# Stores of the FFT's intermediate results, sent from ScalarE's queue instead of SyncE's

## The chip, the cores and the metric

One core of one Trainium2 chip runs the whole program. A core has TensorE (matrix products into PSUM), VectorE, ScalarE and GpSimd, each with its own instruction queue served in order, and SyncE, which only issues transfers. The metric is the device time of one execution in microseconds; three runs of the kernel before gave 601.61, 601.63 and 604.45 us, median 601.63.

## The reference

Two layers follow each other. The first is a global filter: an FFT along the sequence, a product with a complex filter, and the inverse.

```
x: (8, 2496, 256) float32                      # batch, sequence, channels
X = rfft(x, axis=1); Y = X * (filt_r + 1j*filt_i); y = irfft(Y, n=2496, axis=1)
```

The second is a mixture of eight experts; each of the 19968 tokens goes to one of them.

```
logits = y @ w_gate + modality_bias[modality_id]          # y as 19968 rows of 256
e = argmax(logits); gate = softmax(logits)[e]
out[token] = gate * (relu(y[token] @ w1[e]) @ w2[e])      # w1[e]: 256x1024, w2[e]: 1024x256
```

## The kernel before

The FFT of length 2496 is done as 48 x 52 in matrix products, in three stages for each batch of 2496 tokens.

Stage one (`stage1`, L204) multiplies pieces of x by a 96x96 matrix; ScalarE evicts each result from PSUM into a tile t (L214), and after every second eviction, and after the last of a batch, the tile is stored into the DRAM tensor `b1_d` (L217): seven stores a batch. Stage two loads it back in another layout as t2 (`load_t2`, L449), transforms it (`forward`, L464), evicts it on ScalarE into xf (L496), multiplies it on VectorE by the filter (L503, L504), transforms back (`inverse`, L474), and ScalarE evicts into a tile z (L518); after every second eviction z is stored into `b2_d` (L520): six stores a batch. Stage three loads that as t4 (`load_t4`, L455), does the last products (L564, L567), evicts y into yo (L592 on ScalarE, L594 on VectorE), transposes it (L579) and forms the logits. Tiles t and z have two buffers each: an eviction into one waits until the store of its earlier content has landed.

Then the batch is routed (`count`, `place`, `tabled`), GpSimd scatters its rows into `bins_d`, one bin for each expert (L672), and the experts read blocks of 256 rows from there into xs (`load`, L744; the transfer is L750). A block is transposed (L779), multiplied by w1 (L793) with the result evicted on ScalarE into hT (L798), multiplied by w2 (L806), scaled on VectorE (L813) and scattered by GpSimd into the output (L815).

Batches 0 and 1 keep their intermediate results on the chip. For batch 2 from stage two on, and for batch 3 in stage one, the stores start while the FFT runs alone; this part is written in an order fixed by hand, and the flag `alone` is true in it. From about 120 us on `alone` is false: one loop over steps n (L1117) writes, for each step, stage one of one batch, stage two of the one before, stage three of the one before that, some scatters, and one or two quarter steps of the experts. In this loop the order on each engine is set by the framework's planner: it takes the instructions in the program's order but lets one go ahead that is ready sooner by its own estimate of times. PSUM holds three buffers with the tag `ps`, which all three stages take in turn, and two for `hps`.

SyncE issues all hardware-queue transfers of this loop: the loads of xs, t2 and t4 and the stores of t and z. It goes through them in the planner's order, and one that waits holds those behind it. What a transfer waits for is written into the program by the framework: for a store the eviction; for a load of t2 or t4 the landing of the stores that it reads; for a load of xs a free buffer of five and, for the first blocks of a batch, the landing of that batch's scatters. Each hardware-queue transfer also counts up one of eight semaphores, in turn, and waits for the landing of the transfer that used the same one before, eight transfers ago.

Of the kernel before, what the change touches and what calls it, by code (L numbers as in the profile page):

```python
# [29 lines left out]
def kernel(  # L30
# [12 lines left out]
    nc = tc.nc  # L43
# [49 lines left out]
    b1_d = nc.dram_tensor("b1_d", (B, NTT, KA, D), BF16, kind="Internal").ap()  # L93
    b2_d = nc.dram_tensor("b2_d", (B, NS, KB, D), BF16, kind="Internal").ap()
# [19 lines left out]
    EV = 2  # L114
# [74 lines left out]
    st = [dict() for _ in range(B)]  # L189

    def chunk_of(t):
        for c, (t0, t1) in enumerate(TCH):
            if t0 <= t < t1:
                return c, t0, t1

    alone = [True]

    def front(pool, tag, bufs=None):

        if alone[0]:  # L200
            return pool.tile([P, EV, D], F32, tag=tag, bufs=bufs, name="fp")
        return pp.tile([P, EV, D], F32, tag="ps", name="ps")

    def stage1(g, k):  # L204
        t = k * EV
        c, t0, t1 = chunk_of(t)
        xt = xts[g, c]
        ps = front(hp, "hps")
        for i in range(EV):
            mm = nc.tensor.matmul(ps[:KA, i, :], lhsT=w1m, rhs=xt[:, t - t0 + i, :], start=True, stop=True)  # L210
        marks["pe"].append(mm.ins)
        if k % 2 == 0:
            st[g]["t1"] = rp.tile([KA, 2, EV, D], BF16, tag="t1", bufs=2, name="t1")
        nc.scalar.copy(st[g]["t1"][:, k % 2], ps[:KA])  # L214
        if k % 2 == 1 or k == NP - 1:
            n = (k % 2 + 1) * EV
            nc.sync.dma_start(b1_d[g, t + EV - n:t + EV].rearrange("t p c -> p t c"),  # L217
                              st[g]["t1"].rearrange("p a b d -> p (a b) d")[:, :n])

    def input_piece(g, k):  # L220

        stage1(g, k)
        if (k + 1) * EV in [t1 for t0, t1 in TCH]:
            load_x()
# [78 lines left out]
    with tc.manual_schedule():  # L303
# [102 lines left out]
        for s0 in range(0, NS, SPB):  # L406
            for src, dst in ((w2m, a1m), (w2x, a2m)):
# [8 lines left out]
                a = 0  # L416
                if s0 == 0:
                    nc.scalar.copy(dst[:, 0, :], tp[:KB, 0:KB])
                    a = 1
# [87 lines left out]
    def returned(g, k, pz):  # L507

        s = k * EV
        if g < TURNED:  # L510
            if k == 0:
                st[g]["zT"] = turns.tile([P, DC, NTT, KA], BF16, tag="turn", name="zT")
            nc.scalar.copy(st[g]["zT"][:, :, :, 4 * s:4 * (s + EV)],
                           pz[:, 0:DC * EV * KB].rearrange("p (a u t) -> p a t u", a=DC, t=NTT))
            return
        if k % 2 == 0:
            st[g]["z"] = rp.tile([KB, 2, EV, D], BF16, tag="z", bufs=2, name="z")
        nc.scalar.copy(st[g]["z"][:, k % 2], pz[:KB])  # L518
        if k % 2 == 1:
            nc.sync.dma_start(b2_d[g, s - EV:s + EV].rearrange("s p c -> p s c"),  # L520
                              st[g]["z"].rearrange("p a b d -> p (a b) d"))

    NK = NS // EV

    def stage2(g, k):

        if k < NK:
            ps = forward(g, k)
        if k > 0:
            pz = inverse(g, k - 1)  # L530
        if k < NK:
            filtering(g, k, taken(g, k, ps))
        if k > 0:
            returned(g, k - 1, pz)

    def around(g, k, middle):

        if k < NK:
            xf = taken(g, k, forward(g, k))
        middle(lambda: k < NK and filtering(g, k, xf))  # L540
        if 0 < k <= NK:
            returned(g, k - 1, inverse(g, k - 1))

    def stage3(g, k):
# [12 lines left out]
        if k < NPY:  # L557
            t0 = TCH[k // 3][0]
            t4 = st[g]["t4", k // 3]
            ps = front(op, "ops", 2)  # L560
            for i in range(EV):
                a, b = divmod(u0 + i, 3)
                t = 4 * a + b if u0 < NYF else 4 * NYG + i
                mm = nc.tensor.matmul(ps[:, i, :], lhsT=wbm[:, 0, :], rhs=t4[:, t - t0, :],  # L564
                                      start=True, stop=u0 >= NYF)
                if u0 < NYF:
                    mm = nc.tensor.matmul(ps[:, i, :], lhsT=wbm[:, 1 + b, :], rhs=t4[:, 4 * a + 3 - t0, :],  # L567
                                          start=False, stop=True)
            marks["pe"].append(mm.ins)
# [372 lines left out]
    with tc.manual_schedule(engines={ET.PE, ET.Activation, ET.DVE}):  # L942
# [145 lines left out]
        n = -(NP + 2)  # L1088
# [23 lines left out]
    n = opening[0][1] + WAIT  # L1112
# [3 lines left out]
    n = 0  # L1116
# [78 lines left out]
```

## Time and profile before

| | before |
|---|---|
| median of three runs | 601.63 us |
| profiled execution | 604.51 us, of which 602.5 us span |
| TensorE (PE) busy | 511.2 us, 85% |
| ScalarE (ACT) busy | 380.8 us, 63% |
| VectorE (DVE), GpSimd (POOL) | 374.0 us and 370.6 us, 62% each |
| hardware-queue transfers (SyncE) | 41.45 MB, 26.4% of the DMA engines' time |
| GpSimd's transfers | 50.75 MB, 34.2% |
| stores of t, 192 KB and 96 KB | 30 and 5 |
| stores of z, 208 KB | 36 |

The span runs from the first to the last instruction of the profiled execution. Issuing a transfer does not count as busy, so SyncE has no share. The chain that ended last lies 47% on TensorE, 15% on transfers, 9% on GpSimd, 8% on VectorE and 6% on ScalarE. Instructions are named by the line that made them: "t L214" is the eviction into t.

### The profile page before, as it was taken

How to read it: one execution, taken by the hardware profiler on the slowest of the kernel's cores; microseconds unless marked ns; L12 is line 12 of the kernel's file. 1: busy time of each engine (PE TensorE's matmuls, PEld its weight loads, DVE VectorE, ACT ScalarE, POOL GpSimd, SP SyncE). 2: the span in 40 equal slices, each digit the busy share in tenths (PEclk: the TensorE clock that was granted, in tenths of full speed). 3: DMA queues.
4: the chain of work that ended last, by engine and by line, in shares of the span. 5: the costliest groups of instructions: out<-in, count | busy, mean ns of one | idle time of the engine just before them, and what ended most of it. 6: DMA issues, size and time to landing. Idle time of an engine off the chain costs nothing.

```text
span 602.5 us, 16296 instructions
## 1 busy us (share of the span) xinstructions
PE 511.2 (85%) x5115; PEld 460.4 (76%) x5115; DVE 374.0 (62%) x1207; ACT 380.8 (63%) x695; POOL 370.6 (62%) x409
## 2 busy tenths in 40 slices
PE   2678978559776997999798995998999999999990
PEld 2667967448665886888688894887888889999990
DVE  8556978646645768578568875775445445555540
ACT  4678969638555886777586773554566556666660
POOL 8133306727726775677657677777777777555552
PEclk9979989859978999899899999999999999999997
DMA  8999995787488877979647646224434334333320
GB/s 150 181 164 206 211 201 124 157 184 215 101 195 231 201 178 203 244 187 244 209 130 215 184 117 187 81 93 136 143 116 124 118 112 133 107 108 109 99 76 23
DMA packets 69301, 93.29 MB, mean 155 GB/s; under 512 B 11427, under 2 KB 52841, under 8 KB 69059
## 3 DMA queue, kind: packets, MB, share of 16 engines
q0 software_dynamic: 21504, 50.75, 34.2%
q1 hardware_dynamic: 47711, 41.45, 26.4%
q8 instruction: 48, 0.79, 0.5%
q14 instruction: 38, 0.31, 0.2%
HBM read 64.68 MB, written 46.35 MB: 184 GB/s over the span
## 4 chain that ended last, share of the span: by engine, by line
PE 47%; DMA 15%; issue 13%; POOL 9%; DVE 8%; ACT 6%; DVEq 0%; POOLq 0%; SPq 0%; ACTq 0%
PE hps L793 13%; PE ops L806 12%; POOL out_dram L815 6%; DMA out_dram<-osb,meta 4%; PE lt L579 3%; PE ps L564 3%; DMA b_d<-z 2%; PE ps L469 2%; DMA t<-b_d 2%; DMA b_d<-t 2%; ACT t L214 2%; DMA bins_d<-yo,pos_i 2%; PE ps L567 2%; PE pT L779 2%; PE pz L481 2%
## 5 line engine op out<-in xcount | busy, mean ns | idle before, releaser
L798 ACT ACTIVATE hT<-hps 128x512 f16<-128x512 f32 x316 | 188.6, 598 | 129.8 <-PE hps L793 127.5
L815 POOL DMA_INDIRECT out_dram<-osb,meta x158 | 162.2, 1026 | 80.5 <-DVE osb L813 38.1
L793 PE MATMUL hps<-xT,w 128*128 128x256 f16 x1264 | 201.4, 282 | 5.3 <-DVE xT L780 4.9
L672 POOL DMA_INDIRECT bins_d<-yo,pos_i x160 | 163.9, 1025 | 60.9 <-issue 21.5
L806 PE MATMUL ops<-w2sb,hT 128*128 x1264 | 195.9, 276 | 2.4 <-issue 2.2
L793 PEld LDWEIGHTS <-w 128*128 128x128 f16 x1264 | 146.3, 147 | 13.0 <-DVE xT L780 8.1
L806 PEld LDWEIGHTS <-hT 128*128 128x128 f16 x1264 | 124.9, 99 | 18.5 <-issue 3.1
L813 DVE TENSOR_SCALAR osb<-ops,meta 128x256 f32<-128x256 f32 x158 | 69.5, 477 | 42.1 <-DMA out_dram<-osb,meta 21.5
L503 DVE TENSOR_TENSOR p<-xf,g 104x512 f16<-104x512 f16 x96 | 40.7, 424 | 54.6 <-ACT xf L496 54.2
L771 DVE COPY w<-w1sb 128x2048 f16 x79 | 56.6, 716 | 28.1 <-PE hps L793 26.8
L496 ACT CAST xf<-ps 104x512 f16<-104x512 f32 x96 | 57.4, 598 | 4.8 <-PE ps L469 4.5
L780 DVE COPY xT<-pT 128x512 f16<-128x512 f16 x79 | 33.4, 423 | 42.7 <-PE pT L779 41.6
L518 ACT CAST z<-pz 104x512 f16<-104x512 f32 x72 | 43.1, 599 | 14.2 <-PE pz L482 7.6
L144 POOL DMA_DIRECT2D xt<-in_x_dram x32 | 17.6, 552 | 42.2 <-PE fp L210 13.7
L214 ACT CAST t<-ps 96x512 f16<-96x512 f32 x52 | 30.2, 581 | 20.9 <-PE ps L210 17.5
L504 DVE TENSOR_TENSOR xf<-xf,g 104x512 f16<-104x512 f16 x96 | 40.5, 422 | 2.9 <-DVE p L503 0.3
L469 PE MATMUL ps<-t,w2m 104*104 104x256 f16 x192 | 38.8, 285 | 3.1 <-DVE ej L713 1.3
L481 PE MATMUL pz<-p,a1m 104*104 104x256 f16 x144 | 36.9, 280 | 4.8 <-DVE yo L594 2.8
L779 PE MATMUL pT<-ident,xs 128*128 128x128 f16 x316 | 31.2, 222 | 10.4 <-DMA xs<-bins_d 10.2
L579 PE MATMUL lt<-ident,yo 128*128 128x128 f16 x320 | 31.7, 222 | 7.7 <-DVE yo L594 4.9
L588 DVE COPY yT<-lt 128x512 f16<-128x512 f16 x80 | 33.5, 419 | 6.9 <-PE lt L584 5.1
L482 PE MATMUL pz<-xf,a2m 104*104 104x256 f16 x144 | 36.4, 279 | 0.0
(206 smaller groups left out, 722.1 us busy)
## 6 DMA issues: line engine op xcount, KB each, us to landing
xs<-bins_d SPq DMA_DIRECT2D x79, 130.0 KB
xt<-in_x_dram POOLq DMA_DIRECT2D x24, 384.0 KB
b_d<-z SPq DMA_DIRECT2D x36, 208.0 KB
t<-b_d SPq DMA_DIRECT2D x18, 384.0 KB
t<-b_d SPq DMA_DIRECT2D x15, 416.0 KB
b_d<-t SPq DMA_DIRECT2D x30, 192.0 KB
w1sb<-in_moe_w_dram POOLq DMA_DIRECT2D x16, 256.0 KB
w2sb<-in_moe_w_dram POOLq DMA_DIRECT2D x8, 512.0 KB
```

Source lines behind the costliest of these rows:

```text
L469: mm = nc.tensor.matmul(ps[:KB, i, :], lhsT=w2m[:, s + i, :], rhs=st[g]["t2", s // SCH][:, s % SCH + i, :], start=True, stop=True)
L481: nc.tensor.matmul(pz[:KB, i, :], lhsT=a1m[:, s + i, :], rhs=p1[:, i, :], start=True, stop=False)
L496: nc.scalar.copy(xf, ps[:KB])
L579: nc.tensor.transpose(pT[:, i, dc, :], yo[:, ub + i, dc * P:(dc + 1) * P], ident)
L672: ins = nc.gpsimd.indirect_dma_start(out=bins_d[:, :], out_offset=IOA(ap=st[g]["pos"][:rows, t:t + 1], axis=0), in_=st[g]["yw"][:rows, t, ...
L771: cp = nc.vector.tensor_copy(b["w1"].rearrange("p a f -> p (a f)"), w1sb[:, ds(ej, 1)].rearrange("p o a f -> p (o a f)"))
L779: nc.tensor.transpose(pT[:, dc, i, :], xh[:, i, dc * P:(dc + 1) * P], ident)
L793: mm = nc.tensor.matmul(hps[:, k, :], lhsT=b["w1"][:, dc, ft:F:FT], rhs=b["xT"][:, dc].rearrange("p i t -> p (i t)"), start=(dc == 0), sto ...
L798: nc.scalar.activation(b["hT"][:, q * FQ:(q + 1) * FQ, :], hps, AF.Relu)
L806: nc.tensor.matmul(b["ops"][:, i, :], lhsT=b["hT"][:, ft, i * P:(i + 1) * P], rhs=w2sb[:, ds(b["ej"], 1), ft, :], start=(ft == 0 and i == ...
L813: nc.vector.tensor_scalar_mul(osb[:, i, :], b["ops"][:, i, :], gate[:, i, :])
L815: ins = nc.gpsimd.indirect_dma_start(out=out[:, :], out_offset=IOA(ap=b["meta"][:, i, 0:1], axis=0), in_=osb[:, i, :], in_offset=None, bou ...
```

## The change

A helper returns the engine whose queue sends a store: SyncE while the FFT runs alone, ScalarE afterwards. Both stores, L217 and L520 before, go through it. Loads stay on SyncE.

```
     alone = [True]
 
+    def stores():
+
+
+        return nc.sync if alone[0] else nc.scalar
+
@@ stage1
         if k % 2 == 1 or k == NP - 1:
             n = (k % 2 + 1) * EV
-            nc.sync.dma_start(b1_d[g, t + EV - n:t + EV].rearrange("t p c -> p t c"),
-                              st[g]["t1"].rearrange("p a b d -> p (a b) d")[:, :n])
+            stores().dma_start(b1_d[g, t + EV - n:t + EV].rearrange("t p c -> p t c"),
+                               st[g]["t1"].rearrange("p a b d -> p (a b) d")[:, :n])
@@ returned
         if k % 2 == 1:
-            nc.sync.dma_start(b2_d[g, s - EV:s + EV].rearrange("s p c -> p s c"),
-                              st[g]["z"].rearrange("p a b d -> p (a b) d"))
+            stores().dma_start(b2_d[g, s - EV:s + EV].rearrange("s p c -> p s c"),
+                               st[g]["z"].rearrange("p a b d -> p (a b) d"))
```

## Rows read from the trace of the kernel before

**Rows 1.** Stretches: length, busy us (instructions) per engine, granted clock, DMA share, GB/s

```profile
core 0: us, PE busy (x) PEld busy (x) DVE busy (x) ACT busy (x) POOL busy (x), PEclk, DMA share, GB/s
120.00:370.00 250.00, 217.91 (x2075) 193.51 (x2076) 167.81 (x582) 168.03 (x313) 164.80 (x168) 0.94 0.73 190
...
170.00:180.00 10.00, 9.71 (x77) 7.94 (x76) 5.59 (x19) 6.30 (x13) 3.54 (x5) 0.80 0.96 195
...
190.00:200.00 10.00, 9.40 (x77) 7.87 (x78) 5.79 (x17) 5.63 (x11) 7.33 (x8) 0.83 0.87 217
200.00:210.00 10.00, 9.67 (x99) 8.44 (x98) 5.97 (x18) 7.95 (x16) 7.28 (x7) 1.00 0.89 231
```

**Rows 2.** Timeline of TensorE: start, duration, line, tiles, idle time before and its end

```profile
168.69 0.59 PE L210 MATMUL ps<-xt,w1m 96*96 96x256 f16 x2 [5.85 <-ACT z L518]
...
190.00 0.28 PE L564 MATMUL ps<-t,wbm 96*128 96x256 f16 x1 [2.67 <-DMA t<-b_d]
...
241.00 0.28 PE L564 MATMUL ps<-t,wbm 96*128 96x256 f16 x1 [3.39 <-DMA t<-b_d]
```

**Rows 3.** Chain of waits in order of time, 100 to 300: start, us, what

```profile
123.95 3.02 DMA xs<-bins_d
...
163.00 4.96 DMA b_d<-z
...
181.11 4.87 DMA b_d<-z
186.06 3.89 DMA t<-b_d
...
237.02 3.93 DMA t<-b_d
```

**Rows 4.** Timeline of ScalarE at the late stores

```profile
157.05 0.59 ACT L518 CAST z<-pz 104x512 f16<-104x512 f32 x1
...
168.06 0.58 ACT L518 CAST z<-pz 104x512 f16<-104x512 f32 x1 [6.44 <-DMA b_d<-z]
...
169.50 0.59 ACT L214 CAST t<-ps 96x512 f16<-96x512 f32 x1
...
177.64 0.58 ACT L518 CAST z<-pz 104x512 f16<-104x512 f32 x1
...
228.07 0.58 ACT L518 CAST z<-pz 104x512 f16<-104x512 f32 x1
```

**Rows 5.** Timeline of SyncE: start, duration, line, transfer, how many

```profile
162.53 0.37 SPq L750 DMA_DIRECT2D xs<-bins_d  x1
163.00 0.40 SPq L520 DMA_DIRECT2D b_d<-z  x1
163.64 3.46 SPq L750 DMA_DIRECT2D xs<-bins_d  x3
168.37 0.33 SPq L217 DMA_DIRECT2D b_d<-t  x1
168.80 0.44 SPq L520 DMA_DIRECT2D b_d<-z  x1
169.51 0.37 SPq L750 DMA_DIRECT2D xs<-bins_d  x1
171.36 0.30 SPq L217 DMA_DIRECT2D b_d<-t  x1
...
232.52 0.99 SPq L750 DMA_DIRECT2D xs<-bins_d  x2
233.56 0.41 SPq L520 DMA_DIRECT2D b_d<-z  x1
```

**Rows 6.** SyncE's waits, 150 to 190: for whom, us in total, times, longest

```profile
SPq L750 <- DMA bins_d<-yo,pos_i: 11.5, 2, 10.4
```

**Rows 7.** The stores of t: duration ns least/median/most, first and last start

```profile
L217 SPq DMA_DIRECT2D b_d<-t x35: 304/310/464, 84.7 to 315.6; - x35
```

**Rows 8.** Timeline of ScalarE in a quiet stretch

```profile
204.63 0.58 ACT L214 CAST t<-ps 96x512 f16<-96x512 f32 x1
205.11 0.58 ACT L496 CAST xf<-ps 104x512 f16<-104x512 f32 x1
```

**Rows 9.** Timeline of TensorE in the same stretch

```profile
205.75 0.38 PE L579 MATMUL lt<-ident,yo 128*128 128x128 f16 x4
```

## The prediction, on record before the changed kernel ran

> **What bounds the kernel now.** I read the table of stretches first. From 120 to 370 us, where the FFT of batches 3 to 7 runs beside the experts, TensorE is busy 217.91 of 250 us and ScalarE 168.03 [rows 1]. In a quiet stretch of it, 200 to 210, TensorE is busy 9.67 of 10 us at full clock and ScalarE 7.95. So the stretch is TensorE's, and what a change is worth there is read from TensorE's gaps. In the timeline of TensorE three gaps stand out that end on a store or on a load behind one: 5.85 us before 168.69, 2.67 us before 190.00 and 3.39 us before 241.00 [rows 2]. After each the granted clock is low: 0.80 as a mean over 170 to 180 and 0.83 over 190 to 200, against 1.00 at 200 to 210 [rows 1]; that is 1.2 GHz for (1 - 0.80) x 10 / 0.5 = 4.0 us, and for 3.4 us. After the third I take it as after the second.
>
> The chain of waits names what held them: a store of z at 163.00 that took 4.96 us, a store of z at 181.11 (4.87) and behind it a load of t4 at 186.06 (3.89), and a load of t4 at 237.02 (3.93) [rows 3]. ScalarE's timeline says that the data of these stores were there earlier: the z eviction of 157.05 ended at 157.64, that of 177.64 at 178.22, that of 228.07 at 228.65, and the next eviction into z waited 6.44 us for the first store's landing [rows 4]. So these stores left SyncE 5.4, 2.9 and 4.9 us late. SyncE's timeline and its waits say why: its queue is served in order, and a load of xs at 162.53 stood ahead of the z store until the scatters into the bins had landed, 10.4 us [rows 5, 6]; at 181 the load ahead was of t2, at 232.52 again two loads of xs.
>
> **The change part by part.** It moves 28 stores of t (seven for each of batches 4 to 7) and 30 of z (six for each of batches 3 to 7) from SyncE to ScalarE. No byte, no eviction and no matmul changes; stores of the time before the experts stay. The sum is made against the profiled execution, 604.51 us (602.5 of span and 2.0 around it), which is 2.88 above the median of 601.63; I take the sum off the median.
>
> *Gap one.* Issued at 157.7, the z store has landed by 162.7 even if it takes 4.96 us again, while the waiting eviction was due when its predecessors ended, at about 161.6. So up to 5.85 us of gap goes, and the slow clock behind it: 1.3 us to 170 and the 4.0 us above at half speed, worth 2.65. Together 8.5 us. What is late next? Each transfer of the hardware queues waits for the one eight before it on the same semaphore. Counted back in SyncE's order, the eighth before the t store of 171.36 is the xs load of 162.53 [rows 5]. That load still waits for scatters, which don't move; an xs load takes 3.02 us in the chain [rows 3], so this semaphore is free at 165.6 at the earliest, and at 167.5 if it takes the 4.96 of its neighbour. Without the gap the t eviction is done near 163.6 (an estimate: it ended at 170.08, 2 us after the stalled one began [rows 4]). ScalarE would then stand for 2.0 to 3.9 us with evictions behind its store, and TensorE, which has three PSUM buffers of that kind, soon with it; the clock may fall again. So from 8.5 - 3.9 - 2.65 = 1.9 to 8.5; I take 4.
>
> *Gap two.* The z store leaves 2.9 us sooner, and so does the load that waits for it: it lands at 187.05 instead of 189.95, and TensorE's gap began at 187.33. 2.67 go, with 3.4 / 2 = 1.7 of clock: 4.4. The lower end is 0, if something else of that turn of batches is just as late. I take 3.5.
>
> *Gap three.* The store lands by 233.5 even if it takes 4.87 us, but its t4 load stays behind the two xs loads, which keep SyncE until 233.5 [rows 5]. It leaves 3.4 us sooner, which is as much as the gap has: 3.39 + 1.7 = 5.1, lower end 0, taken as 4. Sum of the three: 11.5, between 1.9 and 18.0. Elsewhere I count no gain: no other gap of TensorE in this stretch ends on a store.
>
> *ScalarE.* The trace has no store on this engine; the nearest row is the same store on SyncE, 0.31 us [rows 7]. A store has to wait for the end of its own eviction. In the quiet stretch evictions start 0.48 us apart and last 0.58 [rows 8], so a store directly behind its eviction puts the next one off from 0.48 to 0.58 + 0.31 = 0.89, by 0.41. Behind t comes xf; TensorE's lt transposes at 205.75 need the PSUM buffer that xf leaves at 205.69 [rows 8, 9], so there nearly all 0.41 reaches TensorE: 28 x 0.41 = 11.5. Behind z come yo and hT, whose buffers have more time; half of it, 30 x 0.2 = 6.0. Upper end 17.5. The other end is 0: the planner, which sets ScalarE's order here, may let the xf eviction go first, and then the issue lies under the 0.48 of that eviction; below nothing can't be, as ScalarE loses no work. The cover is thin: ScalarE has 2 us idle in 10. I take 0.1 a store, 5.8 us, nearer the free end because the planner fills an engine with what is ready and xf mostly is.
>
> SyncE's 58 x 0.31 us saved are worth nothing; it waits most of its time. DVE, GpSimd and the DMA engines get the same work, earlier by what TensorE gains.
>
> Sum: -11.5 + 5.8 = -5.7, so 595.9; I say 596. What is gained before 370 us I let through to the end, because GpSimd idles in the same gaps and moves along.
>
> One rule speaks against the gain. In this trace the store of z takes 4.96 and 4.87 us to land with the DMA engines 96 and 87% busy just behind them [rows 1, 3]. The Trainium skill (DMA: Bandwidth & Descriptors, "Issuing engines are not separate DMA queues" and the table of choices at its end) says that DMAs from several engines share the same 16 DMA engines and that spreading them only saves the issuing sequencer's time. By that alone the gain would be 0 and the time 601.6 + 5.8 = 607.4. The trace agrees on the landing times, which I leave as they are, but its gaps come from what stood ahead in the queue, so I hold the rule for half of the story.
>
> **The rivals.**
> *ScalarE pays (slower).* Each store sits directly behind its eviction, 17.5 us, and the semaphore wait of gap one leaves only 8 of the 11.5: 601.6 + 9.5 = 611.1. It decides from 11.5 / 58 = 0.2 us of TensorE time a store. For it: the 0.06 us between xf and lt. Against: the 2 us in 10 in which ScalarE idles. Chance 0.20.
> *The gaps stay (no change).* The loads behind the stores are held by xs loads that wait for scatters, or TensorE meets the next late load instead; 3 us come back, and the stores cost 5.8: 604.4, between 601.6 (as much gained as paid) and 607.4 (nothing gained). For it: 10.4 us of such a wait [rows 6]. Against: at gap two no xs load stands ahead of the store. Chance 0.20. The rule of the Trainium skill above, nothing saved but issue time, ends in this case.
> *All of it.* All three gaps and their clock come back, 18.0: 583.6 with free stores, 589.4 with the 5.8; I put it at 587. Against: the semaphore eight back. Chance 0.10.
> *Forecast.* Gaps mostly close, stores mostly hidden: 596, own range 590 to 600. Chance 0.50.
>
> **How the numbers follow.** I can tell 0.5%, 3 us, from no change. Faster than 598.6: 0.42 of the forecast's 0.50 and the 0.10, 0.52. Slower than 604.6: 0.17 of the first rival and 0.07 of the second, 0.24. The rest, 0.24, is no change. The range runs from 588 to 607: it leaves out the better half of the case with all gains and most of the first rival's upper half, and holds everything between.
>
> **What would show it.** Right: the gap of 5.85 us before TensorE's L210 is gone or under 4 us; the z store of that place starts 0.1 us after its eviction; the t4 loads land before TensorE asks; the issue rows on ScalarE are about 0.3 us with another eviction started before them. Wrong: xf or hT starting 0.9 us after the eviction ahead with TensorE waiting for ps; ScalarE standing microseconds before a store whose own eviction is done; gaps of the old size at the turn of the batches with other names. If the planner orders the other engines anew, no step of this holds alone.

## The result, and the profile after

Four runs of the changed kernel gave a median of 595.19 us (592.68 to 595.93), four of the kernel before in the same session 602.44 (601.61 to 604.45): a ratio of 0.987, 95% interval 0.9838 to 0.9903. The forecast was 596.0. A second comparison on another chip, e9 below, gave 0.9825 (0.9768 to 0.9883); its medians, 597.38 against 604.07 us, would put it at 0.989, from six executions between 589.19 and 600.66 us. I take the gain as between 1 and 2%. So the time was right. Its terms were not: the three gaps gave about 6 us and not 11.5, the issues of the stores cost TensorE nothing that can be seen and not 5.8, and some 3 us of the difference between the two profiles lie in a place that the forecast had not counted.

The profiled execution took 595.62 us, its span 593.4. The page after, busy time first, then the transfer queues; q10 is the hardware queue that ScalarE issues on, q1 is SyncE's.

```profile
PE 511.0 (86%) x5115; PEld 461.3 (78%) x5115; DVE 372.5 (63%) x1207; ACT 380.4 (64%) x695; POOL 371.5 (63%) x409
...
q1 hardware_dynamic: 24409, 29.94, 19.7%
q10 hardware_dynamic: 23302, 11.50, 7.5%
```

The work is the same. 11.50 of the 41.45 MB have moved to the other queue, and the two queues together take 27.2% of the DMA engines' time where one took 26.4%: nothing became cheaper to carry. The stretches of [rows 1], the same times from the start; the work in them is some 4 to 6 us further on from 163 on:

```profile
120.00:370.00 250.00, 220.77 (x2102) 196.72 (x2103) 171.57 (x600) 169.83 (x317) 172.41 (x176) 0.94 0.76 195
170.00:180.00 10.00, 9.05 (x73) 7.39 (x72) 6.94 (x30) 6.07 (x14) 2.30 (x2) 0.88 0.87 226
```

TensorE's gaps after, in its timeline (the number in brackets is the idle time before the instruction, and what ended it). Line numbers are 5 higher than before: L215 is L210, L474 is L469, L569 is L564.

```profile
168.71 0.38 PE L474 MATMUL ps<-t,w2m 104*104 104x256 f16 x2 [2.10 <-ACT z L523]
...
182.71 0.67 PE L474 MATMUL ps<-t,w2m 104*104 104x256 f16 x2 [2.39 <-DMA t<-b_d]
...
236.25 0.28 PE L569 MATMUL ps<-t,wbm 96*128 96x256 f16 x1 [3.10 <-DMA t<-b_d]
...
283.45 0.27 PE L486 MATMUL pz<-p,a1m 104*104 104x256 f16 x1 [1.55 <-DVE yo L599]
```

Against [rows 2] the gap of 5.85 us has become one of 2.10, the gap of 2.67 on a t4 load has become one of 2.39 on a t2 load, and that of 3.39 is nearly unchanged. A gap of 0.89 us on a t2 load (before 232.05) has become one of 1.81 (before 227.25). Two gaps of before that stand in no group there, in the same view:

```profile
185.03 0.42 PE L469 MATMUL ps<-t,w2m 104*104 104x256 f16 x2 [1.29 <-DVE ej L713]
...
289.13 0.27 PE L481 MATMUL pz<-p,a1m 104*104 104x256 f16 x1 [2.79 <-DVE yo L594]
```

Where the time came back is read best by counting one kind of instruction: the k-th eviction of t is the same work in both kernels. I take its start from ScalarE's timeline and count from batch 3 on, whose 13 pieces run while the FFT is alone; the 14th is the first of batch 4.

| eviction of t | before | after | after - before |
|---|---|---|---|
| 14th | 128.96 | 129.05 | +0.1 |
| 24th | 160.55 | 160.94 | +0.4 |
| 25th, behind gap one | 169.50 | 163.49 | -6.0 |
| 28th | 182.29 | 178.62 | -3.7 |
| 31st, behind gap two | 194.87 | 189.16 | -5.7 |
| 32nd | 197.51 | 191.80 | -5.7 |
| 40th | 227.59 | 221.82 | -5.8 |
| 45th, behind gap three | 243.12 | 237.73 | -5.4 |
| 58th | 286.16 | 281.73 | -4.4 |
| 59th | 294.10 | 286.73 | -7.4 |
| 61st | 302.03 | 293.36 | -8.7 |

How late a store leaves can be counted too, from the end of the last eviction that it carries to its own start. Before, eight stores of t and z leave more than 1.5 us late, 11.8 us at the most; in the changed kernel two do, by 3.65 and 2.64 us.

### The profile page after: what moved, and what is told of

It is laid out like the page before. It is cut to its first block, busy times and chain, and to the rows that moved or that the text cites. A ratio compares the mean times of both kernels' runs of the same rounds, so it can differ in the third digit from the quotient of the medians.

```text
span 593.4 us, 16261 instructions
## 1 busy us (share of the span) xinstructions
PE 511.0 (86%) x5115; PEld 461.3 (78%) x5115; DVE 372.5 (63%) x1207; ACT 380.4 (64%) x695; POOL 371.5 (63%) x409
## 3 DMA queue, kind: packets, MB, share of 16 engines
q10 hardware_dynamic: 23302, 11.50, 7.5%
## 4 chain that ended last, share of the span: by engine, by line
PE 45%; DMA 15%; issue 15%; DVE 10%; POOL 9%; ACT 3%; DVEq 1%; POOLq 0%; SPq 0%; ACTq 0%
PE hps L798 12%; PE ops L811 11%; POOL out_dram L820 7%; DMA out_dram<-osb,meta 5%; DMA t<-b_d 3%; PE ps L474 3%; PE lt L584 3%; PE ps L569 2%; DMA bins_d<-yo,pos_i 2%; PE pz L486 2%; PE pz L487 2%; DMA b_d<-t 2%; PE ps L572 2%; DVE osb L818 2%; PE pT L784 1%
## 5 line engine op out<-in xcount | busy, mean ns | idle before, releaser
L474 PE MATMUL ps<-t,w2m 104*104 104x256 f16 x192 | 39.7, 290 | 7.4 <-DMA t<-b_d 4.5
```

The source lines that it names most:

```text
L474: mm = nc.tensor.matmul(ps[:KB, i, :], lhsT=w2m[:, s + i, :], rhs=st[g]["t2", s // SCH][:, s % SCH + i, :], start=True, stop=True)
```

## The experiments

The theory to test (order): the time was lost because SyncE's queue is served in order and loads of xs that wait for scatters stood ahead of stores whose data was ready. Its rivals: a second hardware queue carries the same bytes better (queue), SyncE has fewer transfers to issue (issue time), and the forecast's own price on ScalarE (price). A fourth, named ahead of e1, is that the planner's other order of TensorE, ScalarE and VectorE made the gain; the table speaks against it, since the difference moves at the gaps and stays within 0.4 us from the 31st to the 42nd eviction.

Two helpers appear in the diffs. `marks["st"]` notes each store. `behind(name, n)`, which the kernel has, makes the planner place an instruction after the n-th last one noted under that name; this is an order for the planner and no wait on the chip.

**e2: the order alone, on one queue.** The kernel before, all stores on SyncE, each xs load placed behind the last store.

```
-            nc.sync.dma_start(b1_d[...   # and the same for b2_d
+            ins = nc.sync.dma_start(b1_d[...
+            marks["st"].append(ins.ins)
-        ld = nc.sync.dma_start(xs, ...)
+        with behind("st", 1):
+            ld = nc.sync.dma_start(xs, ...)
```

> The kernel before, all stores on SyncE, with each load of xs held on SyncE behind the stores that stand before it in the program. Theory Q: the store of z leaves within 0.5 us of its eviction, the gap of 5.85 us before L210 is gone, and most of the change's gain or more comes without ScalarE: 590 to 597. Rival H: one hardware queue as before, so no gain: 601 to 604. Rival S (it matters that SyncE has fewer transfers to issue): 601 to 604 too.

Measured: 596.99 us, ratio 0.9907 (0.9871 to 0.9943). SyncE's timeline, and the gap that is left on TensorE:

```profile
160.34 0.31 SPq L521 DMA_DIRECT2D b_d<-z  x1
161.16 3.30 SPq L753 DMA_DIRECT2D xs<-bins_d  x3
164.57 0.40 SPq L217 DMA_DIRECT2D b_d<-t  x1
```

```profile
169.76 0.61 PE L782 MATMUL pT<-ident,xs 128*128 128x128 f16 x4 [4.55 <-DMA xs<-bins_d]
```

The store of z is no longer behind the xs load of 161.16, and the gap on z is gone; now the xs loads come late and TensorE stands 4.55 us for one. More than half of the gain is there (0.0093 of 0.013 to 0.0175) with one queue and as many issues on SyncE as ever. That the second queue or the saved issues were the whole cause falls with this; that the whole gain is order isn't shown, since 0.9907 is a little short of 0.987 and 0.9825. Three stores still leave more than 1.5 us late here, one of z by 6.79 us.

**e4 and e10: one kind of store alone.** e4 is the changed kernel with the stores of t back on SyncE, e10 with those of z back.

```
e4   -            stores().dma_start(b1_d[...
     +            nc.sync.dma_start(b1_d[...
e10  -            stores().dma_start(b2_d[...
     +            nc.sync.dma_start(b2_d[...
```

> Only the stores of z go to ScalarE, those of t stay on SyncE. Theory Q: the three late stores of the prediction were z, so the gain stays, and the two stores of t that held ScalarE for 3.65 and 2.64 us no longer do: 592 to 596. Rival: late stores of t hold the next loads of t2 as much, and half of the gain is theirs: 598 to 600. Rival P: anywhere, without relation to the late stores.

> Only the stores of t leave from ScalarE; those of z stay on SyncE, in their old places behind the loads of xs. Queue order theory, with what the run with z alone showed (a ratio of 1.0016, the late stores of t took the place of the late stores of z): if late stores of either kind hold up TensorE, this one leaves the gap of 5.85 us on z and gains the part of t only, 600 to 604 us. If the late stores of t were the whole of the loss, it gains all of it, 594 to 597 us. Issue price theory: 28 instead of 58 stores on ScalarE change nothing that can be measured here.

Measured: e4 603.60 us, ratio 1.0016 (0.9985 to 1.0047); e10 604.55 us, ratio 0.9999 (0.9965 to 1.0033). Neither gains anything. For e4 that was a miss: it was to keep the gain of gap one. For e10 it lies 0.55 us above the 600 to 604 expected. TensorE, SyncE and ScalarE in e4:

```profile
174.25 0.24 PE L589 MATMUL lt<-wg,yT 128*128 128x8 f16 x4 [9.61 <-ACT t L219]
...
239.22 0.39 PE L569 MATMUL ps<-t,wbm 96*128 96x256 f16 x1 [7.12 <-DMA t<-b_d]
```

```profile
160.84 4.49 SPq L755 DMA_DIRECT2D xs<-bins_d  x4
166.73 0.34 SPq L222 DMA_DIRECT2D b_d<-t  x1
```

```profile
173.62 0.58 ACT L219 CAST t<-ps 96x512 f16<-96x512 f32 x1 [9.77 <-DMA b_d<-t]
```

The t store of 166.73 carries the evictions of 151.42 and 154.19; the second ended at 154.77, so the data lay ready 12.0 us. The next pair, of 158.19 and 160.75, went into the other buffer, and its store left at 168.42, 7.1 us late. The eviction of 173.62 needs the first buffer again and waited 9.77 us for the landing, and TensorE for the PSUM buffer, 9.61 us. In e10 it is z that waits, again behind xs loads; the store of 164.03 carries the eviction of 147.55 and is 15.9 us late (TensorE, SyncE, and ScalarE's z eviction that waits for the tile):

```profile
167.82 0.59 PE L215 MATMUL ps<-xt,w1m 96*96 96x256 f16 x2 [8.37 <-ACT z L523]
```

```profile
161.06 2.87 SPq L755 DMA_DIRECT2D xs<-bins_d  x3
164.03 0.39 SPq L525 DMA_DIRECT2D b_d<-z  x1
```

```profile
167.18 0.58 ACT L523 CAST z<-pz 104x512 f16<-104x512 f32 x1 [8.97 <-DMA b_d<-z]
```

So both kinds of store stood in the same jam, side by side; freeing one leaves the other to end last. In the kernel before, too, the t store of 168.37 left 11.7 us after its data were ready, beside the z store of 163.00. The halves don't add: 0 and 0 make 7 to 11 us.

**e11: a looser order on one queue.** As e2, but behind the fourth last store.

```
-        with behind("st", 1):
+        with behind("st", 4):
```

> All stores stay on SyncE, but each load of xs waits in the written order only for the fourth last store, not for the last one. Queue order theory: between the kernel before (1.0) and the one with the loads behind the last store (0.9907); if the loads of xs then go early enough for TensorE and the stores are still ahead of those that matter, it keeps the gain without the new gap of 4.55 us on xs, 592 to 596 us; if the order falls back to that of before, 601 to 604 us. A second hardware queue as the cause: 601 to 604 us in any case.

Measured: 600.77 us, ratio 0.995 (0.9918 to 0.9982), a third of the gain. TensorE:

```profile
171.88 1.08 PE L796 MATMUL hps<-xT,w 128*128 128x256 f16 x8 [2.49 <-ACT hT L801]
...
177.43 0.67 PE L470 MATMUL ps<-t,w2m 104*104 104x256 f16 x2 [3.81 <-DMA t<-b_d]
```

The gap on xs is gone and gaps on ScalarE and on a t2 load are there instead. On one queue someone has to stand behind the other, loads of xs or stores; the looser order got a third of the gain, and whether e2's got all of it isn't settled. In the changed kernel loads and stores don't stand in one queue; what still ties them is the semaphore eight transfers back.

**e3: the price of a store on ScalarE.** Every eviction of ScalarE is placed behind the last store, so that each store follows its own eviction directly and nothing covers its issue.

```
-        nc.scalar.copy(st[g]["t1"][:, k % 2], ps[:KA])
+        with behind("st", 1):
+            nc.scalar.copy(st[g]["t1"][:, k % 2], ps[:KA])
...      # the same for xf, z, yo and hT
```

> The changed kernel, with every later eviction on ScalarE held behind the store before it, so that a store sits directly behind its own eviction with nothing started in between. The prediction's upper price, 0.41 us of TensorE time for each of 28 stores of t and 0.2 for each of 30 of z: 595 + 17.5 = 612. If ScalarE's idle time before each hT covers the stores anyway: 595 to 598. In between, the price a store is (time - 595) / 58.

Measured: 594.25 us, ratio 0.9865 (0.982 to 0.9909). ScalarE in its quiet stretch, then TensorE at the same time:

```profile
204.22 0.58 ACT L220 CAST t<-ps 96x512 f16<-96x512 f32 x1
204.83 0.31 ACTq L223 DMA_DIRECT2D b_d<-t  x1
205.24 0.59 ACT L504 CAST xf<-ps 104x512 f16<-104x512 f32 x1 [0.44 <-PE pz L489]
```

```profile
205.62 0.60 PE L818 MATMUL ops<-w2sb,hT 128*128 x4
```

The uncovered store puts the next eviction off by somewhat more than the forecast had worked out: xf starts 1.02 us behind t where [rows 8] has 0.48 and the forecast 0.89, with 0.44 of it idle. TensorE does not notice. The row names pz as what ended that wait, but that product of L489 ended at 204.84 and xf reads another tile; what ended just before xf was the store's issue, at 205.14. Between t's and xf's evictions TensorE has products of the experts to do, and it does them. The order of e3 is another one elsewhere as well (its gap at the turn near 285 is 0.48 us), so its median alone would not exclude a price of a few us.

**e9 and e12: twice as many stores on ScalarE.** e9 is the changed kernel again, e12 the same with each ScalarE store cut into two halves, 116 issues in place of 58.

```
+            for h in range(1 if alone[0] else 2):
+                w = n if alone[0] else n // 2
-            stores().dma_start(b1_d[g, t + EV - n:t + EV]...
+                stores().dma_start(b1_d[g, t + EV - n + h * w:t + EV - n + (h + 1) * w]...
...      # the same for b2_d
```

> The changed kernel itself, on the same chip and in the same rounds as the next three, so that they can be compared with it. Queue order theory and its rivals alike: a ratio of 0.987 to the kernel before, as in the first comparison (0.9838 to 0.9903), some 594 to 596 us.

> The changed kernel with every store on ScalarE cut in two, so that ScalarE issues 116 in place of 58 and the bytes stay the same. The forecast's price of 0.1 us a store makes it 5.8 us slower than the changed kernel of the same rounds, its upper bound of 17.5 us for 58 stores as much as 17.5 us slower. If the issues lie beside idle time of ScalarE or under other work of TensorE, as the traces so far show, within 1.5 us of it.

Measured: e9 597.38 us, ratio 0.9825 (0.9768 to 0.9883); e12 597.70 us, ratio 0.9889 (0.9847 to 0.9931). The medians are 0.3 us apart, the ratios 0.0064, 3.9 us, with intervals that overlap: 17.5 us for 58 stores is excluded, 0 and 5.8 are not told apart by this pair. What e12 does show is the wait that the forecast feared, at full size. ScalarE, SyncE and TensorE:

```profile
156.56 0.59 ACT L525 CAST z<-pz 104x512 f16<-104x512 f32 x1
165.21 0.88 ACTq L529 DMA_DIRECT2D b_d<-z  x2
166.13 1.08 ACT L807 ACTIVATE hT<-hps 128x512 f16<-128x512 f32 x2 [8.98 <-DMA b_d<-z]
```

```profile
161.43 5.32 SPq L759 DMA_DIRECT2D xs<-bins_d  x5
```

```profile
166.78 1.01 PE L802 MATMUL hps<-xT,w 128*128 128x256 f16 x4 [7.14 <-ACT hT L807]
```

The z eviction ended at 157.15, and the two stores behind it stood until 165.21 because the first of them shares a semaphore with the first of these xs loads, whose landing the trace has at 165.18. Everything behind it on ScalarE stood too, 8.98 us, and TensorE 7.14. More transfers in the queues moved the count of eight onto an xs load that waits for scatters.

**e1: xs loads behind the stores, in the changed kernel.** An attempt at a better version: the planner places the xs loads after the last store noted, so that no store of gap one counts back to a load held by scatters.

```
+        for m in marks["st"][-1:]:
+            tc.add_manual_dep(ld.ins, m.name, ..., reason="behind stores")   # NoSync: an order, no wait
```

> The changed kernel, with each load of xs placed by the planner behind the stores that stand before it in the program; so the eighth transfer before a store is no longer a load of xs that waits for scatters. Theory Q (what counts is what a store stands behind; what is left of the first gap comes from the semaphore eight transfers back): TensorE's gap of 2.10 us before 168.71 goes, the one of 2.39 us before 182.71 shrinks below 1, and with the slow clock behind it 4 to 6 us come back: 589 to 591. Rival P (the gain came from the other order that the planner gave TensorE, ScalarE and VectorE): no relation to these gaps, 595 give or take 2. Rival H (a second hardware queue moves data sooner): 595, unchanged.

Measured: 592.45 us, ratio 0.9839 (0.9796 to 0.9881): not to be told from the changed kernel's 0.987 and 0.9825. The gap of 2.10 us is gone, as expected. The one behind it was to shrink below 1 us and has grown to 5.17, and 589 to 591 us were missed. Chain of waits and TensorE:

```profile
167.67 10.11 DMA b_d<-t
177.84 4.46 DMA t<-b_d
```

```profile
182.34 0.67 PE L475 MATMUL ps<-t,w2m 104*104 104x256 f16 x2 [5.17 <-DMA t<-b_d]
```

The t store, the last of its batch and so of 96 KB, leaves 0.03 us after its eviction, and then takes 10.11 us to land among three xs loads of 163.69 to 166.03, GpSimd's scatters and its loads of x. The DMA engines' share is 1.02 from 168 to 172 and 0.94 from there to 178: what the queue no longer holds back, they do.

One more comparison is in these runs. e1 and e2 were measured beside each other, both with the xs loads placed behind the last store, and differ, but for the way in which the planner is told, only in the queue that the stores leave from: ScalarE's in e1, SyncE's in e2. e1 is faster, 592.45 against 596.99 us, by 0.0068 in the ratios (0.0012 to 0.0124, an estimate from the two intervals). So with that order the second queue does give something. In e1 no store leaves more than 1.5 us late, in e2 three do, so this too can be order; that the transfers themselves went better nothing here shows.

**e5 to e8: the four kernels of e9 to e12 on another chip.** These ran before e9 to e12, on a chip on which the kernel before itself took 715.09 us and TensorE stood again and again for times that the profile doesn't explain.

> Only the stores of t go to ScalarE, those of z stay on SyncE. Theory Q, after the run with z alone, whose late stores of t held TensorE for 9.61 us: either kind left behind the loads is enough to stop TensorE, since each has two buffers. So the first gap is back, 4 to 10 us ending on ScalarE's z, and the time is 599 to 604. Rival T (the stores of t are the ones that matter, those of z are bystanders): 594 to 597.

> All stores on SyncE, each load of xs held only behind the fourth last store before it in the program, not behind the last. Theory Q: the stores before the first gap leave within half a microsecond of their evictions, and the loads of xs leave as soon as the scatters have landed, about 4 us sooner against TensorE than with the order behind the last store, so the gap of 4.55 us on xs goes too: 590 to 595, without ScalarE and with one hardware queue. Rival H (the second queue gives a good part of the gain): not better than the order behind the last store, 596 to 599.

> The changed kernel once more, beside the others on their chip: 594 to 597, as before. It is the mark for the other three.

> The changed kernel with each store of t and z that goes to ScalarE cut into two transfers of half the size: some 58 more issues on ScalarE, the same bytes. If an issue costs TensorE 0.1 us, as the prediction took: 595 + 5.8 = 601. If it costs nothing because the planner lays TensorE's work around it, as the run with each store directly behind its eviction says: 594 to 598, with the semaphore of eight transfers back as the one thing that could hold ScalarE more often. At the upper price, 0.3 us an issue: 612.

Measured there: t alone 715.87 us, ratio 1.0021 (0.9974 to 1.0067); behind the fourth store 717.92, 1.0064 (1.0013 to 1.0115); the changed kernel 710.58, 0.9962 (0.9925 to 0.9999); split 708.86, 0.9908 (0.9869 to 0.9947). One of ten such gaps of TensorE of 1 us and more, in the changed kernel there; on the first chip it has one, of 1.12 us:

```profile
106.36 0.59 PE L584 MATMUL lt<-ident,yo 128*128 128x128 f16 x4 [6.14 <-issue]
```

With waits of this kind all over the profiles, these four say little about the change, and I draw nothing from them but that the split was not slower there either (by 1.7 us of the medians it was faster), the other way round than in e12.

The stretch from the 14th to the 61st eviction of t, from one profile of each kernel, leaves out the start, which differs by up to 6.4 us between these profiles, and the end:

| kernel | 14th | 61st | between |
|---|---|---|---|
| before | 128.96 | 302.03 | 173.1 |
| after, first profile | 129.05 | 293.36 | 164.3 |
| e9, the same kernel | 126.7 | 293.7 | 167.0 |
| e1, xs behind stores | 129.9 | 289.4 | 159.5 |
| e2, order on SyncE | 123.5 | 289.5 | 166.0 |
| e3, nothing covers a store | 126.3 | 291.2 | 164.9 |
| e4, z alone | 126.7 | 297.7 | 171.0 |
| e10, t alone | 126.5 | 299.9 | 173.3 |
| e11, behind the fourth | 123.6 | 290.6 | 167.0 |
| e12, split | 126.9 | 293.8 | 166.9 |

Two profiles of one kernel differ by 2.7 us here (after and e9), so differences of that size between single profiles mean nothing; e4 and e10 lie 4 us and more above the other changed kernels, as their medians do. e1's 159.5 is the best, but its median doesn't bear it out.

## Why the prediction was right, step by step

*What bounds the stretch.* Right. TensorE's gaps on late stores were the loss: e2 gets more than half of it back by order alone.

*How late the stores were.* The forecast read one of three wrong. A store carries two evictions, and z has two buffers, so the z eviction that waits until 168.06 needs not the tile filled last but the one before it. The z store ahead of 163.00 left at 144.39, so that of 163.00 carries the evictions of 147.46 and 150.59; that of 157.05 left with the store of 168.80. ScalarE before:

```profile
150.59 0.59 ACT L518 CAST z<-pz 104x512 f16<-104x512 f32 x1
```

It ended at 151.18, so the store was 11.8 us late and not 5.4. The 2.9 and 4.9 of the others hold. The sum did not suffer: issued at 151.2, the store lands by 156.2 even if it takes 4.96 us, well ahead of the 161.6 at which the waiting eviction was due; the forecast had 162.7. The jam was twice as long as the forecast had it.

*Gap one, forecast 4 of at most 8.5.* Right, and by the step that was named for it. ScalarE there, after:

```profile
163.49 0.58 ACT L219 CAST t<-ps 96x512 f16<-96x512 f32 x1
163.97 0.58 ACT L501 CAST xf<-ps 104x512 f16<-104x512 f32 x1
167.72 0.31 ACTq L222 DMA_DIRECT2D b_d<-t  x1
168.07 0.59 ACT L523 CAST z<-pz 104x512 f16<-104x512 f32 x1 [3.52 <-DMA xs<-bins_d]
```

The t eviction was to be done near 163.6 and was at 164.07; its store was to stand 2.0 to 3.9 us for the xs load eight transfers back, here that of 163.70, and left 3.65 after the eviction's end; z stood behind it for 3.52 and TensorE for the 2.10 above. The next t store, at 173.12, waited 2.64 us in the same way for the xs load of 165.78. The chain of waits:

```profile
165.78 7.26 DMA xs<-bins_d
173.12 4.79 DMA b_d<-t
177.97 4.69 DMA t<-b_d
```

The xs loads still wait for scatters, SyncE now 13.0 us at the longest where [rows 6] has 10.4, but no store stands behind them on their own engine. By the table the 25th eviction comes 6.0 us sooner, and after these two waits 3.7 are left.

*Gap two, forecast 3.5.* The gap that was to go went, and so did the one of 1.29 before it; in their place TensorE waits 2.39 us at 182.71 for the t2 load at the end of the chain just shown. Between the 28th and 31st eviction 2.0 us come back. The forecast's lower end, "something else of that turn of batches is just as late", is nearer the truth than its value. The clock, too, came back less than forecast:

```profile
168.00:172.00 4.00, 3.29 (x21) 2.69 (x21) 0.41 (x3) 2.64 (x5) 1.35 (x2) 0.62 0.94 174
183.00:187.00 4.00, 4.00 (x25) 3.41 (x24) 1.57 (x8) 2.25 (x4) 3.09 (x4) 0.62 1.02 236
```

These are windows of the kernel after, columns as in [rows 1]. Behind the gaps of 2.10 and 2.39 us the granted clock is 0.62: about 3 of 4 us at 1.2 GHz ((1 - 0.62) x 4 / 0.5), where the gap of 5.85 had brought 5.3 (1.3 and 4.0 in the forecast's working). A gap of a third of the length kept more than half of its slow clock.

*Gap three, forecast 4.* Wrong: nothing came back. This is the step that failed, in the words "it leaves 3.4 us sooner, which is as much as the gap has". The chain of waits after:

```profile
229.56 0.44 SPq L753
...
231.03 5.18 DMA t<-b_d
```

The t4 load left at 231.03, 5.99 us before the 237.02 of [rows 3], but 4.5 of these were the earlier gains, by which TensorE's own gap began sooner too (233.15 against 237.61). The last z eviction that it reads ended at 222.89, and its store left at 222.92 and landed at 228.64, so what held the load after that was not the store but SyncE's queue (leaving at 228.64 and with 5.18 us to land, an estimate, it would have left a gap of 0.7 us):

```profile
222.31 0.58 ACT L523 CAST z<-pz 104x512 f16<-104x512 f32 x1
```

Its waits from 222 to 232 show the xs loads (for whom, us in total, times, longest):

```profile
SPq L755 <- DMA bins_d<-yo,pos_i: 5.8, 2, 3.2
```

They left at 228.16 only, and the register reads for further xs loads (L753), to 230.9, came behind them. So the t4 load gained 1.5 us on TensorE, and lost 1.25 again by landing in 5.18 instead of 3.93. Loads stay on SyncE in this change, and so did this wait; e4 and e10 have the gap at 7.12 and 7.55 us, e9 at 5.07, and of the kernels with another order e3 at 1.23 and e1 at 1.83. A t2 load is later as well: TensorE's gap on it grew from 0.89 to 1.81 us, and from the 40th to the 45th eviction the gain falls by 0.4:

```profile
221.55 5.65 DMA t<-b_d
```

*ScalarE, forecast 5.8, bounds 0 and 17.5.* The lower bound was right. The issue itself was sized right at 0.31 us, the row that answers to [rows 7]:

```profile
L222 ACTq DMA_DIRECT2D b_d<-t x28: 311/312/684, 131.3 to 307.0; - x28
```

From the 32nd to the 40th eviction of t, a stretch without such gaps, before takes 227.59 - 197.51 = 30.08 us and after 221.82 - 191.80 = 30.02: the stores in it cost TensorE nothing. The same stretch takes 30.18 us in e9, 29.60 in e3 without cover and 28.00 in e12 with twice the issues. The mis-sized part is how much of a late eviction reaches TensorE. I took xf against lt in one turn of the PSUM buffers as typical. In the changed kernel another eviction stands between each of the 28 stores of t and its own, and the eviction behind the store starts 0.54 us after the one in front of it (median). e3 takes all cover away, has 0.54 us where the forecast had 0.41, and is no slower than the changed kernel; in the rows above the planner gives TensorE other products meanwhile.

*Elsewhere, forecast nothing.* Wrong by 2.9 us. The chain of waits before and then after, at the turn near 285:

```profile
284.02 4.37 DMA out_dram<-osb,meta
```

```profile
279.61 3.10 DMA out_dram<-osb,meta
```

A scatter into the output took 3.10 in place of 4.37 us to land, VectorE came sooner to yo, the next piece of both chains, and TensorE's gap there is 1.55 in place of 2.79. Behind it the clock of before was low and that of after was not (one window of each):

```profile
289.10:294.00 4.90, 4.87 (x32) 4.05 (x32) 3.39 (x18) 2.34 (x4) 3.31 (x4) 0.65 0.66 209
```

```profile
283.00:288.00 5.00, 4.55 (x44) 4.22 (x44) 4.64 (x21) 3.55 (x7) 3.85 (x6) 1.00 0.88 276
```

1.24 of gap and (1 - 0.65) x 4.90 = 1.7 of clock make 2.9. That the change made this scatter land sooner is not shown. The gap is smaller in other kernels too: 1.28 us in e9, 0.48 in e3, 1.66 in e2, 1.92 in e1, and 1.42 in e4, which gains nothing overall. There is one profile of the kernel before, and it ran 2.07 us over its median; the 2.9 us may be this profile's own and not the change's. Around this place 1.0 us was lost from the 45th to the 58th eviction and 1.3 came back from the 59th to the 61st, where a gap of 1.01 us is gone; neither is explained.

*The rule of the Trainium skill.* Landing did not become quicker: 4.79 us for the t store above and 10.11 for that in e1, both of 96 KB, against 4.96 for the 208 KB of z in [rows 3]. The Trainium skill (DMA: Bandwidth & Descriptors, "Issuing engines are not separate DMA queues") says that spreading DMAs over engines saves only issuing time. On the landing these rows agree with it; as a forecast of the time it failed, 0.987 and 0.9825 in place of no gain. A transfer's time as the kernel sees it begins when its data is ready and not when it is issued: the z store of 163.00 landed 4.96 us after its issue and 16.8 after its data.

*The rivals.* "ScalarE pays" happened nowhere as an issue price, but e12 has its second half, 8.98 us of evictions behind a store that waits. "The gaps stay" is true of gap three and of half of gap two. "All of it" fell at gap one by the semaphore eight back, as argued, and at gap three by SyncE's queue. Two of the signs named for a wrong forecast came: ScalarE stood 3.52 us before a store whose own eviction was done, which the forecast had also counted in gap one, and at gap two there is a gap of nearly the old size with another name. Of the signs of being right one did not come: the t4 load of gap three lands 3.10 us after TensorE asks. So 4 + 2 + 0 + 3 and a price of 0, about 9 us by the two profiles, stand where 4 + 3.5 + 4 - 5.8 = 5.7 was written; the profiled execution of before lies above its medians (604.51 against 602.44 and 604.07), which put the gain at 7.3 and 6.7 us. If the 3 are that profile's own, the 6 of the gaps are what is left, near these two. The time was met because the misses of gaps two and three and of the price cancel, and that is luck.

What stays open: how much of the gain, beyond e2's 0.9907, needs the second queue (e1 against e2 says some of it, with that order); whether 58 more issues cost TensorE 0 or a few us; why the scatter near 280 lands sooner.

## What to carry to other kernels

Measure a store's lateness from the end of what produced its data to its issue, not from issue to landing: if a load ahead of it in the same queue waits for something else, the order in the queue is the cost, and a second issuing engine, or another order, takes it away without a byte less to move. Free all kinds of transfer that stand in the same jam together, since one kind alone may gain nothing, and expect the next late load to take a good part back. A store on a computing engine cost nothing here by its issue, as TensorE had other work meanwhile; what it did cost is the wait in front of it, which held everything behind, so look at what it shares a semaphore with.

## What the runs showed of the hardware that was not expected

A store directly behind its own eviction left ScalarE idle for 0.44 us before the next one (e3, median of 27 stores of t); with another eviction between, in the changed kernel, the median is no idle time (28 stores of t). A 96 KB store took 10.11 us to land in e1 among xs loads and scatters, with the DMA engines' share at 0.94 to 1.02, against 4.79 at 173.12 in the changed kernel. A store on ScalarE stood up to 8.06 us (e12, 157.15 to 165.21) for the landing of a load on SyncE's queue that shares its semaphore. One chip ran all four kernels given to it, and the kernel before, 18 to 20% slower than the others (715.09 against 602 to 604 us), with TensorE idle for up to 6.83 us at a time (e6) on nothing that the profile shows.
